# Attention with a Mish branch on one core: dense query and output rows by DMA, a third bank for ACT, patterns written over each other

## Chip, cores and metric

The kernel runs on one core of one Trainium2 chip. The metric is the device time of one execution in microseconds (us). Lower is better. PE is TensorE, ACT is ScalarE, DVE is VectorE, POOL is GpSimd, and SP is SyncE, which issues most of the DMAs.

## What is computed

The input x has 2048 tokens of 640 features. Branch A is softmax attention with 32 heads of 20 dimensions. Branch B is a dense layer to 1536 features, Mish, and a dense layer back. A gate per token mixes the two.

```python
g = _sigmoid((x * gate_w).sum(-1, keepdims=True))
qkv = (x @ wqkv)                                    # 640 -> 3 * 640, 32 heads of 20
scores = jnp.einsum("bhqd,bhkd->bhqk", q, k) * Dh ** -0.5
a = (softmax(scores) @ v) @ wo
h = x @ w1 + b1
b = (h * tanh(log1p(exp(-abs(h))) + where(h > 0, h, 0))) @ w2
out = g * a + (1 - g) * b
```

## The kernel before

**Tiles.** The tokens form 4 chunks c of 512 queries and 16 key tiles kt of 128 keys. The 32 heads form 8 groups g of 4 heads j. A unit is one (c, g, kt, j): a score matmul of 32 rows by 128 keys by 512 queries into one PSUM bank, then the exponential of 128x512 numbers. There are 2048 units. A head has 20 dimensions, and is held in KT and QT in a slot of 32 partitions, so that the four heads of a group use the four row strips of PE side by side. Groups run in this order: for chunks 0 and 1, group by group, both chunks in turn; then chunk 2 with all groups, then chunk 3.

**Who does the exponentials.** ACT takes two units at once (`emit_e`, line 1096), from two banks of PSUM into the ring ETS of 15 banks. The PSUM banks are two sets of three (0 to 2 and 3 to 5), of which the two first of each set hold ACT's scores; bank 6 (ACC) accumulates the PV products, and the banks FLEX (7, 5, 2) serve everything else. VectorE takes whole key tiles of four units: the conversion at line 1151 (`emit_x`) maps a score straight to the bits of a half-precision number, which approximates its exponential; then two more patterns with shifted bits are made from the first one (line 1178, 128x2048 each). The three patterns are multiplied with V in three weights, added up in ACC by `pv` (line 1298), with the weighted copies VS of V made by POOL (`weigh`, line 1201). A pattern occupies one of the lines LN, or a spare part of W2R, REG or HB, until PE has read it; the third pattern overwrites the first one where PE has already read that.

**The order of the work.** The program is written out at build time by a planner (`Plan.add`), with estimated costs of each instruction, one list for each engine. A step of the loop emits an exponential, the scores for two steps later (`compose`, `emit_s`), perhaps a conversion for VectorE (`x_block`, `emit_x`), the PV products that are ready (`emit_pv`, `emit_off`), pieces of projection tasks in between (`pick`, `put`), and filling matmuls where PE would be streaming too little (`fill_up`). `start_tile` decides whether VectorE begins a new tile: it needs free lines (one, and up to two more for unfinished patterns), VectorE not too far behind (BEHIND), and from slot CALM on; where a group has too little left, a tile is taken from the next group, its key tiles 0 and 1 only. `room` holds tiles back if VectorE's outstanding work is above LOAD times the time left. A slot is three units. Engines wait for each other by semaphores, in the order of their lists, and SP issues its DMAs in order as well.

**Projections.** Queries (`kq_task`, line 559) are computed group by group and chunk by chunk from weights that POOL has copied into padded columns (`pad`, line 537), five matmuls of 512 columns each, so that the four heads land in their 32-partition slots; VectorE evicts them (line 571). Keys of groups 1 to 7 are already computed in dense rows of 128 (`k_task`, line 613), evicted into a line of LN, written by DMA into the DRAM tensor KS (`shelve`, line 589), and read back in slots (line 605). The first queries and keys have code of their own (`first_keys`, line 681). V is at lines 707 and 734.

**Finishing a group.** After the last PV product of a group, `group_done` copies ACC to OUNG (line 1385), sends the row sums through three DMAs on SP (line 1388 into RR, a reciprocal at line 1392, lines 1393 and 1395 into BCT through the DRAM tensor SUMS), and multiplies OUNG by BCT (`times`, line 1355) into QT, over the queries of that group and chunk, which nobody needs any more. So the attention output lies in padded slots too: 4 x 32 partitions for a group. The output projection (`p_mm`, line 937) therefore takes 8 passes, one for each group, against Wo in padded rows (WOG), for each 128 tokens and each half of 320 columns. `load_wo` (lines 817 and on) fills WOG by nine DMAs when the last query task is done. For chunk 3, groups 0 to 5 are summed early (`part_task`, into PART), and groups 6 and 7 at the end (`late_mm`). VectorE mixes the result with branch B (line 943).

**Branch B.** The first layer is line 852, bias line 862, the tanh of Mish on ACT line 886, four VectorE pieces lines 903 to 906, the second layer lines 913 and 920.

## Time and profile before

| quantity | us |
|---|---|
| time before, median of 3 runs | 797.2 (796.22 to 799.04) |
| time of the profiled execution | 796.31 |
| span in that profile, first to last instruction | 794.5 |
| busy in it: PE / DVE / ACT / POOL | 774.7 / 681.7 / 772.9 / 146.2 |

The granted clock of PE was 0.999 in this execution. Groups of instructions are shown as line, engine, operation, output <- input, shapes, and xcount, then busy time, mean duration in ns, and the idle time of the engine ahead of them with what ended it. Durations overlap where an engine pipelines: 808 exponentials of a mean of 1119 ns keep ACT busy for 749.6 us. In timelines a row begins with start and length. In tables by stage each engine has its busy time and the count of its instructions, and the last three columns are the granted clock, the DMAs' share and GB/s. A "slice" of the span is a fortieth.

### The profile page before, as it was taken

What the parts mean: (1) busy time and instruction counts of PE and PEld (TensorE: products, weight loads), DVE (VectorE), ACT (ScalarE), POOL (GpSimd) and SP (SyncE); (2) the same over time, 40 slices, a digit from 0 to 9 for tenths busy, and PEclk for the clock granted to TensorE, in tenths of its full rate; (3) what the DMA queues carried; (4) which work ended last, traced back from release to release, by engine and by line L of the source; (5) the groups of instructions that cost most, each with busy time, mean ns of one, the idle gap of its engine ahead of it and who ended that gap; (6) DMA issues with size and microseconds to landing.
All of it is one profiled execution on the core that took longest, in us unless ns stands there. A gap on an engine that the chain in (4) does not pass through costs nothing.

```text
span 794.5 us, 16928 instructions
## 1 busy us (share of the span) xinstructions
PE 774.7 (98%) x7139; PEld 276.7 (35%) x7139; DVE 681.7 (86%) x1080; ACT 772.9 (97%) x839; POOL 146.2 (18%) x253
## 2 busy tenths in 40 slices
PE   8999999999999999999999999999999999999996
...
DMA packets 70020, 42.54 MB, mean 54 GB/s; under 512 B 20616, under 2 KB 65920, under 8 KB 69888
## 3 DMA queue, kind: packets, MB, share of 16 engines
...
q14 instruction: 26, 0.21, 0.1%
...
## 4 chain that ended last, share of the span: by engine, by line
ACT 67%; PE 27%; DVE 3%; DMA 1%; issue 0%; SPq 0%
ACT ETS L1096 64%; PE PS L1069 10%; PE PS L1298 8%; PE PS L559 2%; ACT REG L886 2%; PE PS L852 2%; PE PS L734 1%; PE PS L913 1%; DVE LN L1151 1%; PE PS L613 1%; PE PS L937 1%; DMA LN<-in_A_x_dram 1%; ACT W2R L886 1%; DMA RR<-OUNG 1%; PE PS L632 0%; DVE LN L1178 0%
## 5 line engine op out<-in xcount | busy, mean ns | idle before, releaser
L1096 ACT ACTIVATE ETS<-PS 128x1024 bf16<-128x1024 f32 x808 | 749.6, 1119 | 6.6 <-PE PS L1069 3.6
L1069 PE MATMUL PS<-QT,KT 32*128 32x512 bf16 (+1 forms) x2126 | 326.8, 377 | 11.0 <-ACT ETS L1096 7.3
L1151 DVE TENSOR_SCALAR LN<-PS 128x512 int16<-128x512 f32 x336 | 226.3, 683 | 25.7 <-PE PS L1069 24.0
L1201 POOL TENSOR_SCALAR VS<-V_all 128x84 bf16<-128x84 bf16 x224 | 131.1, 585 | 400.1 <-PE PS L1298 326.0
L1069 PEld LDWEIGHTS PS<-QT,KT 32*128 32x128 bf16 x2126 | 78.7, 91 | 245.0 <-ACT ETS L1096 215.1
L1298 PE MATMUL PS<-ETS,V_all 128*21 128x512 bf16 (+1 forms) x1664 | 154.0, 376 | 0.3 <-DVE V_all L715 0.3
L1178 DVE TENSOR_SCALAR LN<-LN 128x2048 int16<-128x2048 int16 x134 | 92.0, 690 | 3.4 <-PE PS L1298 2.4
L913 PE MATMUL PS<-W2R,HB 128*128 128x320 bf16 x384 | 76.9, 303 | 0.0
L1298 PEld LDWEIGHTS PS<-ETS,V_all 128*21 128x21 bf16 x1664 | 39.7, 90 | 64.0 <-issue 47.3
L1298 PE MATMUL PS<-LN,VS 128*21 128x512 f16 (+1 forms) x692 | 61.3, 375 | 0.0
L852 PE MATMUL PS<-XB,REG 128*128 128x256 bf16 x360 | 58.1, 275 | 0.0
L937 PE MATMUL PS<-WOQ,QT 128*128 128x320 bf16 x256 | 51.2, 303 | 0.4 <-DVE QT L1378 0.2
L559 PE MATMUL PS<-XB,WOQ 128*128 128x512 bf16 x155 | 48.7, 385 | 0.2 <-DVE V_all L744 0.2
L537 POOL COPY WOQ<-WOQ 128x400 bf16<-128x400 bf16 x16 | 8.3, 524 | 209.5 <-PE PS L559 204.8
L913 PEld LDWEIGHTS PS<-W2R,HB 128*128 128x128 bf16 x384 | 29.4, 97 | 37.2 <-issue 30.5
L852 PEld LDWEIGHTS PS<-XB,REG 128*128 128x128 bf16 x360 | 29.1, 97 | 24.2 <-issue 21.3
L862 DVE TENSOR_TENSOR HB<-PS,B1F 128x512 bf16<-128x512 f32 x48 | 32.7, 682 | 3.0 <-PE PS L852 3.0
L1151 DVE TENSOR_SCALAR REG<-PS 128x512 int16<-128x512 f32 x48 | 32.8, 684 | 1.5 <-PE PS L1069 1.4
L1298 PE MATMUL PS<-LN,V_all 128*21 128x512 f16 (+1 forms) x348 | 33.0, 376 | 0.0
L905 DVE SCALAR_TENSOR_TENSOR U<-U 128x1024 f32<-128x1024 f32 x24 | 29.4, 1224 | 0.1
L937 PEld LDWEIGHTS PS<-WOQ,QT 128*128 128x128 bf16 x256 | 19.5, 97 | 23.9 <-issue 17.4
L571 DVE CAST QT<-PS 128x512 bf16<-128x512 f32 x31 | 21.1, 681 | 7.6 <-PE PS L559 7.5
...
## 6 DMA issues: line engine op xcount, KB each, us to landing
...
```

Of the source, the lines that this page charges most:

```text
L559: return lambda e, bank: e.matmul(PS[:, bank, :], pads[:, b, f, :], xt(c)[:, f, :], start=(f == 0), stop=(f == NFT - 1))
L852: return lambda e, bank: e.matmul(PS[:, bank, i * HW:(i + 1) * HW], w1b(n1)[:, f, i * P:(i + 1) * P], xt(c)[:, f, cols], start=(f == 0), s ...
L862: ev = dve(lambda e: e.tensor_tensor(hb, PS[:, bank, :].rearrange("p (i t) -> p i t", i=2), bias, ALU.add), [last, *b1f, *guarded, *b_read ...
L905: piece(BROAD, lambda e: e.scalar_tensor_tensor(G, G, b, G, ALU.add, ALU.mult))
L913: return lambda e, bank: e.matmul(PS[:, bank, 0:HALF], HB[:, hc % 2, f, t * P:(t + 1) * P], W2[:, f, half * HALF:(half + 1) * HALF], start ...
L937: return lambda e, bank: e.matmul(PS[:, bank, 0:HALF], otn(c, g)[:, t * P:(t + 1) * P], WOG[:, g, half * HALF:(half + 1) * HALF], start=(g ...
L1069: op = pl.add("pe", lambda e, to=to, g=real(g), tile=tile, j=j, cols=cols, c=c, of_q=of_q: e.matmul(to[:, cols], KT[32 * j:32 * j + 32, g, ...
L1096: e_op[s] = pl.add("act", lambda e: e.activation(RING[:, p:p + n, :], scores(s)[:, 0:n, :], AF.Exp, scale=SCALE), [s_op[s], *(pv_slot[b] f ...
L1151: bank_free[bank] = x_ops[bank] = tile["op"] = dve(lambda e: e.tensor_scalar(dst, PS[:, bank, :], SCALE * ULPS, BASE, ALU.mult, ALU.add), ...
L1178: op = pl.add("dve", lambda e: e.tensor_scalar(to, src, SHADES[n], None, ALU.add), [last, *deps], cost=SHADE)
L1201: weighted[(c, g, k)] = n, [pl.add("pool", lambda e, i=i, n=n, src=src: e.tensor_scalar(VS[:, n, i, :, :], src, WEIGHTS[i + 1], None, ALU. ...
L1298: lasts[n] = pl.add("pe", lambda e, v=v, j=j, src=src[:, cols], of_q=of_q, begin=begin, end=end: e.matmul(PS[32 * j:32 * j + EW, ACC, of_q ...
```

## The change

1. **Queries.** Only group 0 is still computed with padded weights. The other 560 query rows are computed in dense rows, four tasks of 128 rows for each chunk, and the last 48 rows for two chunks side by side (`row_task`). VectorE evicts a task into one of two buffers (ROWS), and `send` issues one DMA on SP for each head's rows in it, into that head's slot of QT. POOL clears QT for groups 1 to 7 beforehand (seven memsets). A score matmul waits for the DMAs of its own head.
2. **Outputs.** `times` writes into one of two new buffers (ONS), and DMAs on SP move each head's 20 rows to their dense place in QT, split where they cross a multiple of 128. Wo is loaded dense (WOD, one DMA); the output projection takes 5 passes instead of 8. Groups 6 and 7 of chunk 3 keep padded rows (WOL, four DMAs and a memset by POOL); the early part of chunk 3 takes 4 passes instead of 6.
3. **Third bank.** `third` lets a step's exponential take three units where the third bank of its set is idle: with a conversion in the same step, or with VectorE behind ACT by THIRD; and not where projections press (CALLED).
4. **Patterns.** Each pattern after the first is made from the one before, in place if PE has read that one, or else in a new line if more than SPARED or KEPT lines are free. A new tile needs at most one line more than its own (NEED).
5. **Next group.** A tile of the next group may be any of its first four (BEFORE).
6. **Constants** of the planner are changed, among them CALM (21 to 10), LOAD (1.104 to 0.556), BEHIND (47.3 to 31.0), H_AT (172 to 150), PACKED (14 to 17) and the due times of the late queries.

```diff
-SLACK = 0.205
-LATER = 0.323
-FREE = 0.14
+SLACK = 0.225
+LATER = 1.181
+THIRD = 0.615
+CALLED = 0.642
+ROWED = 2
+SPARED = 0
+KEPT = 2
+NEED = 1
+BEFORE = 4
+FREE = 0.174
...
-AHEAD = 18
-BEHIND = 47.318
-MORE = 4.568
-PATIENCE = 2.597
-CATCH_UP = 289.517
+AHEAD = 19
+BEHIND = 30.956
+MORE = 6.787
+PATIENCE = 4.697
+CATCH_UP = 661.752
...
-SHIFT = 1.018
-LAG = 113
-WINDOW = 1.402
-CALM = 21
-PACKED = 14
-Q_AT = 70
-Q_STEP = 27.078
+SHIFT = 0.798
+LAG = 311
+WINDOW = 4.166
+CALM = 10
+PACKED = 17
+Q_AT = 84
+Q_STEP = 30.0
...
-SQ_STEP = 11
-H_AT = 172
+SQ_STEP = 13
+H_AT = 150
...
-LOAD = 1.104
+LOAD = 0.556
...
+    ONS = sb("ONS", [P, 2, CW], BF16)
...
-    PADQ = WOQ[:, NFT * D:].rearrange("p (b f c) -> p b f c", b=3, c=P)
-    WOG = WOQ[:, :].rearrange("p (g c) -> p g c", c=D)
+    PADQ = WOQ[:, NFT * D:NFT * (D + P)].rearrange("p (b f c) -> p b f c", b=1, c=P)
+    ROWS = [WOQ[:, NFT * (D + P) + n * CW:][:, 0:CW] for n in range(2)]
+    WOD = WOQ[:, 0:NFT * D].rearrange("p (f c) -> p f c", c=D)
+    WOL = WOQ[:, NFT * D:(NFT + 2) * D].rearrange("p (g c) -> p g c", c=D)
...
+            for g in range(1, NG):
+                blank_q[g] = pl.add("pool", lambda e, g=g: e.memset(QT[:, g, :].bitcast(FP32), 0.0), cost=1.2)
...
+            q_rows, row_free, row_read, q_sent = {}, {}, {}, [0]
+
+            def send(base, m, c, src, ev, n):
+
+                at = base
+                while at < base + m:
+                    head = at // DH
+                    g, j = divmod(head, HG)
+                    to = min(base + m, (head + 1) * DH)
+                    first, last = 32 * j + at - head * DH, 32 * j + to - head * DH
+                    name = f"qs{q_sent[0] % 8}"
+                    q_sent[0] += 1
+                    row_read[name] = op = pl.add("sp", lambda e, g=g, first=first, last=last, at=at, to=to: e.dma_start(
+                        QT[first:last, g, c * CW:(c + 1) * CW], src[at - base:to - base, :]),
+                        [ev, blank_q[g], row_read.get(name)], name, cost=0.5)
+                    wq_read.append(op)
+                    row_free.setdefault(n, []).append(op)
+                    some = q_rows.setdefault((g, c, j), [])
+                    some.append((to - at, op))
+                    if sum(rows for rows, _ in some) == DH:
+                        q_done[(g, c, j)] = [op for _, op in some]
+                    at = to
+
+            def row_task(name, parts, due):
+
+                base, m = (HD + P * name, P) if name < 4 else (HD + 4 * P, D - HD - 4 * P)
+
+                def mm(f, i, c):
+                    return lambda e, bank: e.matmul(
+                        PS[64 * i:64 * i + m, bank, :], WQ[:, f, base:base + m], xt(c)[:, f, :],
+                        start=(f == 0), stop=(f == NFT - 1), **(dict(tile_position=(0, 64 * i)) if m < P else {}))
+
+                def finish(bank, last):
+                    wq_read.append(last)
+                    n = row_turn[0] % 2
+                    row_turn[0] += 1
+                    for c in parts:
+                        x_read[c].append(last)
+                    ev = dve(lambda e: e.tensor_copy(ROWS[n], PS[:, bank, :]), [last, *row_free.pop(n, ())], WIDE)
+                    for i, c in enumerate(parts):
+                        send(base, m, c, ROWS[n][64 * i:64 * i + m, :], ev, n)
+                    return ev
+
+                return Task([mm(f, i, c) for f in range(NFT) for i, c in enumerate(parts)], PASS / len(parts), finish, due,
+                            lambda: [*(d for c in parts for d in xt_load[c]), w_load["wq"]], True)
+
+            row_turn = [0]
...
-                pieces = [(f"wo{j}", WOG[32 * j + 1:32 * j + 1 + DH, :, :], wo_v[j], 1.7) for j in range(HG)]
-                pieces.append(("wz", WOQ[0:P:32, :], none.to_broadcast([HG, NG * D]), 0.4))
-                pieces += [(f"wz{j}", WOQ[32 * j + 1 + DH:32 * j + 32, :], none.to_broadcast([32 - EW, NG * D]), 0.9)
-                           for j in range(HG)]
+                wo_v = A_wo[(NG - 2) * HD:, :].rearrange("(g j r) c -> j r g c", g=2, j=HG, r=DH)
+                blank = pl.add("pool", lambda e: e.memset(WOL.bitcast(FP32), 0.0), list(wq_read), cost=0.8)
+                pieces = [("wo", WOD, A_wo.rearrange("(f p) c -> p f c", p=P), 4.0)]
+                pieces += [(f"wo{j}", WOL[32 * j + 1:32 * j + 1 + DH, :, :], wo_v[j], 0.4) for j in range(HG)]
...
+        def p_mm(c, t, half, n, passes):
+
+            g, rows = passes[n]
+            w = WOL[:, g - (NG - 2), :] if rows == 0 else WOD[0:rows, g, :]
+            o = otn(c, g)[0:rows or P, t * P:(t + 1) * P]
             return lambda e, bank: e.matmul(
-                PS[:, bank, 0:HALF], otn(c, g)[:, t * P:(t + 1) * P], WOG[:, g, half * HALF:(half + 1) * HALF],
-                start=(g == groups[0]), stop=(g == groups[-1]))
+                PS[:, bank, 0:HALF], o, w[:, half * HALF:(half + 1) * HALF], start=(n == 0), stop=(n == len(passes) - 1))
...
+        all_rows = [(f, P) for f in range(NFT)]
+        early_rows = [(f, min(P, (NG - 2) * HD - f * P)) for f in range(-(-(NG - 2) * HD // P))]
+        late_rows = [(g, 0) for g in late]
...
+        def third(s, x):
+
+            bank = SLOT * (s % 2) + 2
+            if not fast or s < CALM or x and x[2] == bank or now["open"] and now["home"] == bank or now["rate"] >= CALLED:
+                return 0
+            free = bank_free.get(bank)
+            begin = max(pl.now["pe"], e_op[s - 2].t1 + HOP)
+            late = max(0.0, pl.now["dve"] - pl.now["act"])
+            if not x and late < THIRD or free is not None and free.t1 + HOP > begin:
+                return 0
+            held[bank] = s
+            return 1
+
+        def compose(s, j=None, more=0):
 
             some, js = [], [j]
-            while len(some) < width and order:
+            while len(some) < width + more and order:
...
-            def in_place(n):
-
-                return n == len(SHADES) - 1 and tile["read"]
-
             def ready(n):
+                if tile["read"]:
+                    return max([last, tile["read"]], key=lambda d: d.t1)
                 some = spare()
-                if in_place(n):
-                    return max([last, tile["read"]], key=lambda d: d.t1)
-                return max([last, *line_free[some[0]]], key=lambda d: d.t1) if some else stuck
+                if len(some) <= (SPARED if queue and tile["key"][:2] == queue[0][2][:2] else KEPT):
+                    return stuck
+                return max([last, *line_free[some[0]]], key=lambda d: d.t1)
 
             def piece(n):
                 def run():
-                    at, deps = (tile["at"], [tile["read"]]) if in_place(n) else grab()
+                    held, made = tile["held"], tile["items"][tile["held"]][0]
+                    if tile["read"]:
+                        at, deps = tile["at"], [tile["read"]]
+                        tile["read"], tile["held"] = None, n
+                    else:
+                        at, deps = grab()
                     to = line(at)
-                    op = pl.add("dve", lambda e: e.tensor_scalar(to, src, SHADES[n], None, ALU.add), [last, *deps], cost=SHADE)
+                    op = pl.add("dve", lambda e: e.tensor_scalar(
+                        to, src, SHADES[n] - SHADES[held], None, ALU.add), [made, *deps], cost=SHADE)
                     tile["items"].append((op, at))
                     if n == len(SHADES) - 1:
                         unshaded.remove(tile)
                         tile["shaded"] = op
-                        if at != tile["at"]:
-                            free(tile)
+                        free(tile)
...
-            need = sum(len(SHADES) - 1 - len(t["items"]) for t in unshaded)
+            need = sum(not t["read"] for t in unshaded)
             if (len(order) < 4 * HG or late + urgent + other >= BEHIND
-                    or len(spare()) < 1 + min(max(need, 0), len(SHADES) - 1)):
+                    or len(spare()) < 1 + min(need, NEED)):
...
-                kts = [kt for kt in range(2) if (c, g, kt) not in taken]
-                need = [k_done.get((real(g), 0)), q_done.get((real(g), c))]
+                kts = [kt for kt in range(BEFORE) if (c, g, kt) not in taken]
...
-                oung_free[0] = bc_read[0] = otn_done[(c, g)] = pl.add("dve", lambda e: e.tensor_tensor(
-                    otn(c, g), src, BC, ALU.mult), deps, cost=WIDE)
+                if c == NC - 1 and g in late:
+                    oung_free[0] = bc_read[0] = op = pl.add("dve", lambda e: e.tensor_tensor(
+                        otn(c, g), src, BC, ALU.mult), deps, cost=WIDE)
+                    otn_done[(c, g)] = [op]
+                    return
+                n = norm_turn[0] % 2
+                norm_turn[0] += 1
+                oung_free[0] = bc_read[0] = op = pl.add("dve", lambda e: e.tensor_tensor(
+                    ONS[:, n, :], src, BC, ALU.mult), [*deps, *norm_read.pop(n, ())], cost=WIDE)
+                norm_read[n] = otn_done[(c, g)] = []
+                for j in range(HG):
+                    at = g * HD + j * DH
+                    while at < g * HD + (j + 1) * DH:
+                        to = min((at // P + 1) * P, g * HD + (j + 1) * DH)
+                        first = 32 * j + 1 + at - g * HD - j * DH
+                        name = f"od{len(norm_read[n]) + 5 * n}"
+                        last_od[name] = move = pl.add("sp", lambda e, at=at, to=to, first=first: e.dma_start(
+                            otn(c, at // P)[at % P:at % P + to - at, :], ONS[first:first + to - at, n, :]),
+                            [op, last_od.get(name)], name, cost=0.5)
+                        norm_read[n].append(move)
+                        at = to
...
+            tasks.append(kq_task(0, 0, 1, slot_of(1, 0, 0) - 5))
+            lates = [lambda due, c=c: kq_task(0, 0, c, due) for c in range(2, NC)]
+            for i, g in enumerate((1, 2, 4, 5, NG - 1)):
+                if i < 4:
+                    tasks.extend(row_task(i, (c,), slot_of(c, g, 0) - PACKED - ROWED) for c in range(2))
+                    lates += [lambda due, i=i, c=c: row_task(i, (c,), due) for c in range(2, NC)]
+                else:
+                    tasks.append(row_task(i, (0, 1), slot_of(0, g, 0) - PACKED - ROWED))
+                    lates.append(lambda due, i=i: row_task(i, (2, 3), due))
+            tasks.extend(make(Q_AT + int(Q_STEP * n)) for n, make in enumerate(lates))
...
-                compose(step + 2, x and x[1][3])
+                compose(step + 2, x and x[1][3], third(step + 2, x))
...
```

109 lines of the change are left out of this document (55 added, 54 removed).

## Prediction

> **What bounds the kernel now.** First the busy line and the chain of what ended last, both on the page, and the costliest group.
>
> ```profile
> PE 774.7 (98%) x7139; PEld 276.7 (35%) x7139; DVE 681.7 (86%) x1080; ACT 772.9 (97%) x839; POOL 146.2 (18%) x253
> ...
> ACT 67%; PE 27%; DVE 3%; DMA 1%; issue 0%; SPq 0%
> ...
> L1096 ACT ACTIVATE ETS<-PS 128x1024 bf16<-128x1024 f32 x808 | 749.6, 1119 | 6.6 <-PE PS L1069 3.6 <-PE PS L1298 2.0
> ```
>
> PE and ACT are both near full, and the chain lies on ACT for two thirds. The wait view decides between them: which of the two stands still for the other?
>
> ```profile
> PEld PS L1069 <- ACT ETS L1096: 215.1, 638, 1.1
> ```
>
> The score matmuls' weight loads stand 215.1 us, in 638 places, until an exponential gives its banks back, while ACT waits 6.6 us for PE in all. PE is the follower. So I price ACT's work, from unbroken pieces of the chain in order of time (start, length, what).
>
> ```profile
> 12.92 54.28 ACT ETS L1096 x59
> ...
> 719.56 1.02 ACT REG L886
> 720.58 57.91 ACT ETS L1096 x63
> ```
>
> 57.91 / 63 = 0.919 us for one two-bank exponential, 0.46 us for a unit of 128x512. 808 of them are 742.6 us, and 24 Mish tanhs (8 blocks of 256 tokens, 3 each) at 1.02 us are 24.5: together 767.1 of the 794.5 us span. The other 27.4 us are the head (12.92, in which two exponentials, 1.8 us, already ran: 11.1), the 6.6 us of waits, and by difference 9.7 us of tail. The profiled execution took 796.3 us, 1.8 outside its span; the median before is 797.2, 0.9 above it.
>
> There are 4 x 8 x 16 x 4 = 2048 units. ACT does 1616, so VectorE does 432, which is 108 tiles of four heads. Time comes down almost only by moving tiles to VectorE, by making ACT's units cheaper, or by removing ACT's waits. How much room has VectorE? The busy time by stage (length, then PE, PEld, DVE, ACT, POOL):
>
> ```profile
> 0.00:12.92 12.92, 10.49 (x73) 5.38 (x73) 6.01 (x13) 4.98 (x8) 6.26 (x12) 1.00 0.99 185
> 12.92:40.00 27.08, 26.27 (x227) 9.81 (x227) 5.65 (x11) 27.08 (x30) 3.70 (x9) 1.00 0.45 109
> 40.00:100.00 60.00, 58.92 (x609) 21.15 (x612) 47.71 (x81) 59.90 (x66) 9.06 (x16) 1.00 0.17 49
> 100.00:140.00 40.00, 38.52 (x404) 16.20 (x401) 32.21 (x55) 36.04 (x40) 8.12 (x16) 1.00 0.11 36
> 140.00:340.00 200.00, 197.47 (x1770) 65.42 (x1769) 185.34 (x301) 198.99 (x217) 36.12 (x66) 1.00 0.20 59
> 340.00:740.00 400.00, 394.83 (x3482) 139.92 (x3479) 366.73 (x557) 399.52 (x434) 78.35 (x125) 1.00 0.17 49
> 740.00:784.50 44.50, 44.21 (x550) 17.20 (x550) 34.52 (x62) 44.50 (x49) 3.73 (x8) 1.00 0.06 18
> ```
>
> VectorE is idle 21.4 us before 40, 12.3 and 7.8 in the next two stages, 14.7 and 33.3 in the long ones, 10.0 near the end. So 68.1 us are idle between 40 and 740, and ACT loses 4.0 us in 100 to 140, the one stage where it visibly starves.
>
> **The change part by part.**
>
> *What a tile trades.* Rows of VectorE's timeline, a score conversion, a shifted pattern and a conversion in a row:
>
> ```profile
> 261.46 0.68 DVE L1151 TENSOR_SCALAR W2R<-PS 128x512 int16<-128x512 f32 x1
> 262.06 0.68 DVE L1178 TENSOR_SCALAR LN<-LN 128x2048 int16<-128x2048 int16 x1
> 262.66 0.68 DVE L1151 TENSOR_SCALAR W2R<-PS 128x512 int16<-128x512 f32 x1
> ```
>
> Starts are 0.60 us apart, so a tile (four conversions, two shifted patterns) costs VectorE 6 x 0.60 = 3.6 us and relieves ACT of two exponentials, 1.84 us.
>
> *Queries in rows, outputs in rows.* The groups concerned, and PE's own spacing:
>
> ```profile
> L937 PE MATMUL PS<-WOQ,QT 128*128 128x320 bf16 x256 | 51.2, 303 | 0.4 <-DVE QT L1378 0.2 <-DVE LN L1151 0.2
> L559 PE MATMUL PS<-XB,WOQ 128*128 128x512 bf16 x155 | 48.7, 385 | 0.2 <-DVE V_all L744 0.2
> ...
> L571 DVE CAST QT<-PS 128x512 bf16<-128x512 f32 x31 | 21.1, 681 | 7.6 <-PE PS L559 7.5
> ```
>
> ```profile
> 402.68 0.39 PE L1298 MATMUL PS<-ETS,V_all 128*21 128x512 bf16 x4
> 402.90 0.60 PE L1298 MATMUL PS<-LN,VS 128*21 128x512 f16 x8
> ...
> 404.07 0.72 PE L913 MATMUL PS<-W2R,HB 128*128 128x320 bf16 x4
> 405.90 0.45 PE L913 MATMUL PS<-W2R,HB 128*128 128x320 bf16 x2
> ```
>
> A second 512-column pass adds 0.60 - 0.39 = 0.21 us, a 320-column one (0.72 - 0.45) / 2 = 0.135. Query passes fall from 160 (the 155 and the first five) to 4 x 5 + 16 x 5 + 10 = 110: 50 x 0.21 = 10.5 us off PE. Output passes fall from 256 to 12 x 2 x 5 = 120, plus 8 x 4 and 8 x 2 for the last chunk, 168: 88 x 0.135 = 11.9 us. On PE, which follows, these 22.4 us buy nothing directly. They buy part of the 4.0 us that ACT loses in 100 to 140, where projections crowd the scores; I take 2, between 0 and 4. They also pay for two more PV passes (0.42 us) per tile. VectorE gains directly: query evictions fall from 32 to 1 + 3 + 16 + 2 = 22, 10 x 0.60 = 6.0 us.
>
> The price is DMAs. Query rows cross heads and go out as 7 + 7 + 8 + 7 + 3 = 32 pieces per chunk, 128 in all. Outputs go as 4 or 5 pieces per group, 36 per chunk, less 9 for the two groups kept padded: 135. Nearest row, the K pieces that the kernel already sends so:
>
> ```profile
> L589 SPq DMA_DIRECT2D KS<-LN x20: 314/336/1095, 36.0 to 282.1; - x20
> ...
> DMA to landing us min/median/max: 1.6/1.7/4.8
> ```
>
> Issue 0.336 us, landing 1.7. 263 x 0.336 = 88 us more on SP, spread over 772. Queries are due 19 slots before use and outputs are read by projections planned long after, so I cost both at nothing; the cover is that lead, and the norm chain, which uses the same queue, is the rival below.
>
> Seven clears of QT come onto POOL ahead of its first scaling of V:
>
> ```profile
> 0.72 0.20 POOL L492 MEMSET LN<- 128x128 bf16 x1 [0.29 <-POOLq L1818]
> ...
> 7.05 2.36 POOL L544 MEMSET V_all<- 128x512 bf16 x1
> ...
> 16.39 0.20 POOL L551 COPY REG<-GW 128x5 bf16<-128x5 bf16 x1 [4.67 <-DMA GW<-in_gate_w_dram]
> ...
> 33.74 2.92 POOL L1201 TENSOR_SCALAR VS<-V_all 128x84 bf16<-128x84 bf16 x6
> ```
>
> By elements, 1024 is 8 x 0.20 = 1.6 us by the dense clear and 2 x 2.36 = 4.7 by the strided one: 11 to 33 us after 16.6, ending at 28 to 50. These clears are dense, so I take 1.6. That ends about where the first tile now begins (below), at no cost; at 4.7 the first tiles would wait, at worst some 15 us of VectorE time, once, or 5 us by the balance below. The dropped Q pads give POOL time back, which it doesn't need.
>
> *Third bank.* What does a third bank cost in the same instruction? Two casts of ACT from PSUM give the slope:
>
> ```profile
> L656 ACT CAST XB<-PS 128x512 bf16<-128x512 f32 x2 | 1.2, 585 | 4.7 <-PE PS L672 4.6
> ...
> L656 ACT CAST KT<-PS 128x256 bf16<-128x256 f32 x1 | 0.4, 372 | 1.5 <-PE PS L660 1.5
> ```
>
> 213 ns for 256 columns, 0.426 us a bank. The two-bank exponential is then 0.852 plus 0.067 of its own, and a third bank costs 0.426 where it would cost 0.46: 0.033 us gained each. How often it is taken no row shows; between never and every second exponential (400, 13 us). The bank must be idle of conversions and projections, and the 432 conversions already sit beside half of the steps, so I take 150: 5 us.
>
> The Trainium skill (ScalarE: Activation LUTs, Rules for kernel authors) budgets about 0.3 us for every ACTIVATE beside 0.83 ns per element. Its slope agrees with the casts' 0.832; its fixed part would make two banks 1.15 us, where the run of 63 shows 0.919, so the fixed part is mostly hidden between exponentials in a row. By the page the 150 banks would save half of 0.3 us each, an estimated 22 us instead of 5.
>
> *Overwriting patterns, four early tiles, start at slot 10.* Before, an unfinished tile reserves up to two more lines, and a tile may begin only with a line left over; now a pattern that PE has read is shifted in place, so lines come free sooner and up to four tiles fill a group's end. What VectorE waits for in the long stages:
>
> ```profile
> DVE LN L1151 <- PE PS L1069: 13.2, 29, 1.6
> ```
>
> It is a conversion that had not been started in time, not a late result, so idle time is there to be had. The chain read, shift, read, shift now ties each pattern to PE, which can cost at a group's end. Beginning at slot 10 instead of 21 is 11 x 3 units x 0.46 = 15 us earlier, but PE is 97% busy there. Together I let VectorE win s = 30 us of idle time: 5 of the 21.4 before 40, 25 of the 68.1 after. Bounds: 0 and 75.
>
> *The sum.* With n more tiles, the span falls by d = 1.84 n + 5 (third bank). VectorE must fit 3.6 n - 6.0 into s - d, so n = (s + 6 - 5) / 5.44 = 31 / 5.44 = 5.7. Then d = 10.5 + 5 = 15.5, and with the 2 us of waits 17.5. From the profiled execution's 796.3 that is 778.8, from the median 779.7: **780 us**, about 114 tiles.
>
> **The rivals.**
>
> *VectorE no denser* (s = 0, third bank hardly taken, 1 us): n = 5 / 5.44 = 0.9, d = 2.7, no waits won: 794.5. For it: VectorE is already 92% busy in the two long stages, and the stricter load factor (0.556 for 1.104) holds tiles back in the second half. Against: the 6.0 us of evictions are gone whatever else happens. This is also the case that the edits are planned but not taken.
>
> *VectorE nearly full* (s = 60, third bank 8, waits 3): n = 58 / 5.44 = 10.7, d = 19.6 + 8 + 3 = 30.6: 766.5. For it: 68.1 us idle with no late input behind most of it. The page's 0.3 us would end there too (17 more than 17.5: 763); the run of 63 speaks against that.
>
> *SP's queue* (slower). The norm chain in VectorE's timeline, then in SP's:
>
> ```profile
> 254.31 0.68 DVE L1385 COPY OUNG<-PS 128x512 f32<-128x512 f32 x1
> ...
> 267.57 0.68 DVE L1355 TENSOR_TENSOR QT<-OUNG,BCT 128x512 bf16<-128x512 f32 x1
> ```
>
> ```profile
> 255.01 0.55 SPq L1388 DMA_DIRECT2D RR<-OUNG  x1
> ...
> 258.70 0.34 SPq L1393 DMA_DIRECT2D SUMS<-RR  x1
> 261.55 0.53 SPq L1395 DMA_DIRECT2D BCT<-SUMS  x1
> ```
>
> The chain holds OUNG 13.3 us; a group lasts about 772 / 31 = 24.9. SP works in order: a row DMA that waits for its VectorE result holds these three behind it. If a group's chain grows past 24.9, by more than 11.6 us, the next copy out of ACC waits, PV stops, and the ring of 15 banks holds ACT up. The added issues are 2.9 us per group, so it decides only when waiting in the queue is three times the issuing. At half of the groups, 1.6 us each, it costs 15 x 1.6 = 24 us: 797.2 - 17.5 + 24 = 803.7. The Trainium skill (DMA: Bandwidth & Descriptors, Rules for kernel authors) speaks against such pieces: transfers under 64 KB pay mostly overhead and are to be coalesced, and these have 20 KB or less. The 1.7 us landing of the K pieces agrees that the time is overhead; whether anyone waits for it is this rival.
>
> **How the numbers follow.** Forecast 0.55 (s from 15 to 45, the third bank and the waits between their bounds: 771 to 789); no denser 0.15; nearly full 0.15; SP's queue, or the clears at their upper bound, 0.15. About 0.3% (2.4 us) can be told from no change; 0.06 of the second case lies within it. Faster 0.55 + 0.15 + 0.09 = 0.79, same 0.06, slower 0.15. The range must keep 0.8: 767 leaves out half of the third case, 797 the slower one, so it is 767 to 797; the forecast's own is 771 to 789.
>
> **What would show it.** Right: L1151's count above 432 by some 20 or more; three-bank exponentials at about 1.35 us; VectorE's idle time between 40 and 740 near 40 us; ACT as full as now, with about 36.0 of 40 grown to 38 in 100 to 140. Query evictions 22, output matmuls 168. Wrong: ACT idle for PV or scores spread over the groups (queue or shift chain), SP rows long before the norm chain's three, the copy out of ACC waiting for OUNG, a tile count near 432, or POOL clears of 4 us with PE waiting for VS near 40.

## Result and the profile after

The changed kernel takes 829.2 us (median of 4 runs, 825.23 to 830.27); the kernel before took 798.1 us on the same chip (796.22 to 799.04). The ratio is 1.038, with a 95% interval of 1.034 to 1.043: 31 us slower, where 17 us faster was forecast. The profiled execution took 830.27 us, its span 828.3 us, with a mean granted clock of 0.964.

The page of the changed kernel: busy time, granted clock in fortieths of the span, the chain that ended last, and two groups. The exponential is now line 1170, the scores line 1143, the reciprocal of the row sums line 1494.

```profile
PE 757.0 (91%) x7053; PEld 266.7 (32%) x7087; DVE 703.6 (85%) x1118; ACT 760.6 (92%) x790; POOL 159.6 (19%) x262
...
PEclk9989989999997968998999999999999999999999
...
ACT 62%; PE 24%; DVE 6%; DMA 4%; SPq 1%; issue 1%; ACTq 0%; DVEq 0%
...
L1170 ACT ACTIVATE ETS<-PS 128x1024 bf16<-128x1024 f32 (+1 forms) x759 | 737.5, 1149 | 52.5 <-PE PS L1143 46.8
...
L1494 DVE RECIPROCAL RR<-RR 128x16 f32<-128x16 f32 x31 | 7.7, 248 | 27.8 <-DMA RR<-OUNG 27.8
```

Less work everywhere (PE 757.0 for 774.7, ACT 760.6 for 772.9), and a longer span. ACT's idle time ahead of exponentials went from 6.6 to 52.5 us. The reciprocal is new among the costly groups: VectorE stood 27.8 us for its input, and PE's clock fell in several slices of the first half. In the kernel before, VectorE stood 3.2 us for the row sums; the row of the DMA that brings them, there (ns min/median/max, first and last start), and who waited for it:

```profile
L1388 SPq DMA_DIRECT2D RR<-OUNG x31: 538/560/936, 42.3 to 765.8; - x31
...
  DVE RR L1392: 3.2, 4
```

ACT's groups with shapes kept apart:

```profile
L1170 ACT ACTIVATE ETS<-PS 128x1024 bf16<-128x1024 f32 x691 | 658.1, 1112 | 46.6 <-PE PS L1143 41.3 <-PE PS L1379 4.4
L1170 ACT ACTIVATE ETS<-PS 128x1536 bf16<-128x1536 f32 x67 | 102.4, 1541 | 5.9 <-PE PS L1143 5.5 <-PE PS L1379 0.3
```

With one exponential of a single unit, ACT did 691 x 2 + 67 x 3 + 1 = 1584 units, so VectorE did 464: 116 tiles, 8 more than before. A third bank costs 1541 - 1112 = 429 ns and was taken 67 times. ACT's work is 691 x 0.919 + 67 x 1.348 + 0.6 + 24.5 = 750.4 us, 16.7 less than the 767.1 before: the saving came. The waits by stage ate it (length, then PE, PEld, DVE, ACT, POOL, clock):

```profile
40.00:100.00 60.00, 54.26 (x573) 20.16 (x579) 49.37 (x87) 53.02 (x57) 10.23 (x18) 0.94 0.18 51
100.00:140.00 40.00, 32.98 (x303) 14.53 (x302) 28.03 (x47) 26.10 (x28) 8.15 (x18) 0.87 0.18 56
140.00:340.00 200.00, 182.69 (x1615) 63.72 (x1627) 170.36 (x274) 176.69 (x186) 33.07 (x54) 0.92 0.19 53
340.00:740.00 400.00, 377.82 (x3408) 128.21 (x3408) 368.56 (x561) 392.61 (x407) 77.29 (x119) 0.99 0.20 58
```

ACT is idle 7.0 + 13.9 + 23.3 + 7.4 = 51.6 us between 40 and 740, against 5.6 before, almost all of it ahead of 400. That is where the query pieces stand in SP's queue. Their row and that of the output pieces (ns min/median/max, first and last start):

```profile
L672 SPq DMA_DIRECT2D QT<-WOQ x128: 549/707/1701, 38.0 to 374.7; - x128
...
L1453 SPq DMA_DIRECT2D QT<-ONS x135: 558/714/932, 61.8 to 793.8; - x135
```

A piece of 20 rows holds SP for 0.71 us, twice the 0.336 of the K pieces of 128 rows. One spell shows what follows. Timelines of SP, VectorE, PE and ACT from 275 us on:

```profile
275.12 4.00 SPq L1453 DMA_DIRECT2D QT<-ONS  x5
279.18 5.20 SPq L672 DMA_DIRECT2D QT<-WOQ  x7
284.43 1.18 SPq L615 DMA_DIRECT2D KT<-KS  x2
285.65 0.48 SPq L865 DMA_DIRECT2D W2R<-in_B_w_dram  x1
286.17 0.58 SPq L1490 DMA_DIRECT2D RR<-OUNG  x1
286.79 0.65 SPq L865 DMA_DIRECT2D W2R<-in_B_w_dram  x1
287.50 6.11 SPq L672 DMA_DIRECT2D QT<-WOQ  x7
...
280.61 0.69 DVE L1487 COPY OUNG<-PS 128x512 f32<-128x512 f32 x1 [0.23 <-PE PS L1379]
...
291.60 0.25 DVE L1494 RECIPROCAL RR<-RR 128x16 f32<-128x16 f32 x1 [4.30 <-DMA RR<-OUNG]
...
291.42 1.25 PE L908 MATMUL PS<-XB,W2R 128*128 128x256 bf16 x5 [3.65 <-DMA W2R<-in_B_w_dram]
...
293.24 1.02 ACT L1170 ACTIVATE ETS<-PS 128x1024 bf16<-128x1024 f32 x1 [4.25 <-PE PS L1143]
```

Twelve pieces hold SP from 275.12 to 284.38. The copy to OUNG ended at 281.30, but its row sums leave SP at 286.17, 4.9 us later; in the rows that the prediction shows of the kernel before, the copy ended at 254.99 and they left at 255.01. Keys, weights of w1 and row sums leave together, behind the pieces; the weights land 5.7 us after 285.65, and PE stands 3.65 us and VectorE 4.30, each at the head of an in-order list. Over the 31 groups, the row sums left 37.0 us in all after their copy had ended (8.5 at most); in the kernel before it was 0.8 us. And it isn't over when they land. The same stretch by the granted clock:

```profile
283.00:287.50 4.50, 4.50 (x48) 1.30 (x46) 3.97 (x6) 4.50 (x6) 0.00 (x0) 1.00 0.16 46
287.50:291.40 3.90, 0.27 (x3) 0.00 (x0) 0.00 (x0) 1.50 (x2) 0.00 (x0) 0.93 0.79 193
291.40:304.60 13.20, 13.18 (x72) 3.75 (x72) 9.19 (x13) 6.92 (x7) 0.00 (x0) 0.50 0.19 55
304.60:311.00 6.40, 6.40 (x62) 2.27 (x58) 5.20 (x9) 6.30 (x7) 0.00 (x0) 1.00 0.07 21
```

After a stand of 3.65 us PE is granted half its clock for 13.2 us, though it is busy without a break: 72 matmuls in 13.2 us, where it did 48 in 4.5 before. ACT, full until then, is busy 6.92 of the 13.20. By the trace's clock records there are eight such spells ahead of 740 us, 58 us in all; the kernel before has none. Just ahead of six of them an engine had stood for a DMA that SP issues: VectorE for row sums ahead of those that begin at 133.8, 256.7, 290.8, 352.3 and 379.6 us, PE for keys ahead of 106.5. For PE's wait ahead of 51.9 the profile names no cause, and ahead of 318.1 PE waited only for ACT, 0.76 us at the longest.

### The profile page after: what moved, and what is told of

It reads as the page before. It is cut to its first block, busy times and chain, and to the rows that moved or that the text cites. A ratio compares the mean times of both kernels' runs of the same rounds, so it can differ in the third digit from the quotient of the medians.

```text
span 828.3 us, 17267 instructions
## 1 busy us (share of the span) xinstructions
PE 757.0 (91%) x7053; PEld 266.7 (32%) x7087; DVE 703.6 (85%) x1118; ACT 760.6 (92%) x790; POOL 159.6 (19%) x262
## 4 chain that ended last, share of the span: by engine, by line
ACT 62%; PE 24%; DVE 6%; DMA 4%; SPq 1%; issue 1%; ACTq 0%; DVEq 0%
ACT ETS L1170 60%; PE PS L1143 8%; PE PS L1379 7%; DMA RR<-OUNG 2%; ACT REG L942 2%; DVE LN L1228 2%; PE PS L969 1%; PE PS L792 1%; PE PS L908 1%; DVE LN L1258 1%; PE PS L688 1%; SPq L672 1%; PE PS L997 1%; PE PS L623 1%; DMA KT<-KS 1%
## 5 line engine op out<-in xcount | busy, mean ns | idle before, releaser
L1170 ACT ACTIVATE ETS<-PS 128x1024 bf16<-128x1024 f32 (+1 forms) x759 | 737.5, 1149 | 52.5 <-PE PS L1143 46.8
L1143 PE MATMUL PS<-QT,KT 32*128 32x512 bf16 (+1 forms) x2132 | 317.3, 388 | 48.9 <-ACT ETS L1170 33.0
L1228 DVE TENSOR_SCALAR LN<-PS 128x512 int16<-128x512 f32 x352 | 237.2, 684 | 41.8 <-PE PS L1143 39.8
L1283 POOL TENSOR_SCALAR VS<-V_all 128x84 bf16<-128x84 bf16 x240 | 145.4, 606 | 581.4 <-PE PS L1379 376.6
L1258 DVE TENSOR_SCALAR LN<-LN 128x2048 int16<-128x2048 int16 x159 | 108.9, 692 | 7.9 <-PE PS L1379 7.5
L1379 PE MATMUL PS<-LN,VS 128*21 128x512 f16 (+1 forms) x772 | 73.5, 390 | 3.5 <-DVE LN L1258 3.4
L997 PE MATMUL PS<-WOQ,QT 128*128 128x320 bf16 (+1 forms) x168 | 32.7, 302 | 0.3
L1494 DVE RECIPROCAL RR<-RR 128x16 f32<-128x16 f32 x31 | 7.7, 248 | 27.8 <-DMA RR<-OUNG 27.8
L1379 PEld LDWEIGHTS PS<-LN,VS 128*21 128x21 bf16 x772 | 17.8, 90 | 36.6 <-issue 19.7
L688 PE MATMUL PS<-XB,WOQ 128*128 128x512 bf16 (+1 forms) x88 | 25.1, 391 | 1.4 <-issue 0.7
L908 PE MATMUL PS<-XB,W2R 128*128 128x256 bf16 x120 | 22.3, 305 | 3.8 <-DMA W2R<-in_B_w_dram 3.6
```

The lines of the kernel that those rows point to most:

```text
L688: return lambda e, bank: e.matmul(PS[64 * i:64 * i + m, bank, :], WQ[:, f, base:base + m], xt(c)[:, f, :], start=(f == 0), stop=(f == NFT ...
L908: return lambda e, bank: e.matmul(PS[:, bank, i * HW:(i + 1) * HW], w1b(n1)[:, f, i * P:(i + 1) * P], xt(c)[:, f, cols], start=(f == 0), s ...
L997: return lambda e, bank: e.matmul(PS[:, bank, 0:HALF], o, w[:, half * HALF:(half + 1) * HALF], start=(n == 0), stop=(n == len(passes) - 1))
L1143: op = pl.add("pe", lambda e, to=to, g=real(g), tile=tile, j=j, cols=cols, c=c, of_q=of_q: e.matmul(to[:, cols], KT[32 * j:32 * j + 32, g, ...
L1170: e_op[s] = pl.add("act", lambda e: e.activation(RING[:, p:p + n, :], scores(s)[:, 0:n, :], AF.Exp, scale=SCALE), [s_op[s], *(pv_slot[b] f ...
L1228: bank_free[bank] = x_ops[bank] = tile["op"] = dve(lambda e: e.tensor_scalar(dst, PS[:, bank, :], SCALE * ULPS, BASE, ALU.mult, ALU.add), ...
```

## The experiments

**Theory:** the pieces hold SP's in-order queue, so that row sums, keys and weights leave late; VectorE and PE, also in order, stand for them, and PE's granted clock halves behind such stands. **Rivals:** the filling matmuls or the order of the work under the new constants; the outputs' pieces; the bytes of the pieces rather than their issue; or dense query rows as such, which change what PE and VectorE do and when.

Each run is set against the kernel before on its own chip, with medians of 796.3 to 797.1 us there, and 798.1 beside the changed kernel. So "over before" is the difference to that median; the changed kernel is 31.1 us over before.

| kernel | median us | ratio to before (95%) |
|---|---|---|
| before + dense queries (b_q) | 825.0 | 1.035 (1.028 to 1.042) |
| before + dense outputs (b_out) | 795.2 | 0.998 (0.997 to 1.000) |
| before + overwriting patterns (b_pat) | 814.3 | 1.022 (1.018 to 1.026) |
| changed, padded queries (padded_q) | 811.8 | 1.019 (1.014 to 1.024) |
| changed, padded outputs (padded_out) | 832.0 | 1.044 (1.039 to 1.049) |
| changed, both padded (no_rows) | 816.3 | 1.025 (1.019 to 1.031) |
| the same, old constants (no_rows_old) | 815.8 | 1.024 (1.022 to 1.027) |
| changed, WINDOW as before (window) | 848.8 | 1.065 (1.058 to 1.073) |
| changed, pieces planned at 0.73 (told) | 831.2 | 1.043 (1.038 to 1.049) |
| changed, one row in each piece (one_row) | 815.8 | 1.024 (1.018 to 1.031) |
| the same for queries only (one_row_q) | 818.2 | 1.027 (1.019 to 1.036) |
| changed, pieces issued by POOL (pool_pieces) | 803.8 | 1.010 (1.005 to 1.015) |
| before + 128 idle pieces (ballast) | 817.4 | 1.030 (1.023 to 1.036) |
| before + 256 idle pieces (ballast_2) | 901.8 | 1.132 (1.126 to 1.138) |
| changed, queries through DRAM (qs_raw) | 813.1 | 1.020 (1.017 to 1.022) |
| the same, constants fitted anew (qs_2) | 806.9 | 1.012 (1.010 to 1.014) |
| changed, padded queries, constants fitted anew (pq_2) | 793.2 | 0.994 (0.992 to 0.996) |

### Which row edit

**padded_q**: the queries of the kernel before in the changed kernel; no query pieces, no clears.

```diff
-                tasks.extend(row_task(i, (c,), slot_of(c, g, 0) - PACKED - ROWED) for c in range(2))
...
+                        tasks.append(kq_task(0, g, c, first - 5 if c < 2 else 70 + int(27.078 * (2 * g + c - 2))))
```

> The changed kernel with the padded queries of before (32 tasks of five 512-column passes, pads copied by POOL, no query rows by DMA); all else as changed. The queue theory says: the 128 query pieces of 0.71 us each stand ahead of the norm chain, the key fetches and the weight loads on SP in the first 390 us. Without them VectorE's 27.8 us of waits for the row sums fall to under 10, ACT's 47 us of waits for scores to under 15, the half-clock spells (granted clock 0.964) nearly go (over 0.985), and the time is 790 to 805 us. The dense-plan theory (VectorE packed to 116 tiles with no slack, so that any jitter stalls PE) says the waits stay above 30 us and the time stays above 815. The filler theory (the longer window lets PE stream too little) says the same, with the clock still near 0.965.

811.8 us, 14.8 over before: 16 us of the 31 went, but the time is outside the 790 to 805 of the theory. The reciprocal's wait fell to 0.6 us, the mean clock rose to 0.997, ACT's waits fell to 20.6. So the stalls for SP's DMAs are gone with the query pieces. But the time isn't back: 14.6 of the 20.6 us are waits for PV products, and 14.6 us of span follow the last exponential, where the changed kernel and the one before have less than 9.

**padded_out**: the outputs of the kernel before in the changed kernel.

```diff
-                if c == NC - 1 and g in late:
+                if True:
```

> The changed kernel with the padded output rows of before (no output pieces by DMA, Wo in padded rows, 256 output matmuls); query rows by DMA stay. The queue theory says: half of the 135 output pieces go from the first 390 us, while the 128 query pieces stay, so perhaps a third of the waits goes: 808 to 822 us, clock 0.97 to 0.985. If the query pieces alone matter it stays at 822 to 830. The dense-plan and filler theories: no gain, or slower by the 12 us of PE passes, 825 to 840.

832.0 us, ACT's waits 48.1, and 10.4 us for the last wait of all. The output pieces do add to the queue: without them the row sums left 20.9 us late in all instead of 37.0, and the reciprocal waited 10.1. But the time did not fall, so they alone are not the cause. They are issued behind the three DMAs of their own group's row sums, four or five for each group, and so stand ahead of what the next group needs.

**b_q** and **b_out**: one row edit alone on the kernel before, with its constants. (The diffs are parts 1 and 2 of the change.)

```diff
+                tasks.extend(row_task(i, (c,), slot_of(c, g, 0) - PACKED - ROWED) for c in range(2))
```

> The kernel before with the dense query rows by DMA alone (row tasks, 128 pieces on SP, seven clears by POOL), and its old constants. By the queue theory these pieces alone bring waits of VectorE for the row sums over 10 us and half-clock spells before 390 us: 803 to 815. By the prediction's account (10 fewer evictions, 10 us less of PE, pieces at nothing): 790 to 796.

```diff
+                    ONS[:, n, :], src, BC, ALU.mult), [*deps, *norm_read.pop(n, ())], cost=WIDE)
```

> The kernel before with the dense output rows by DMA alone (135 pieces on SP, 168 output matmuls for 256). The queue theory: pieces are issued just after the multiplication, when no norm chain is under way, so little harm: 792 to 800. If they hold the next key fetch and weight load up, 800 to 812.

Dense queries alone cost 28 us, more than the theory's 803 to 815, with ACT's waits at 27.8, the reciprocal's at 9.2, row sums 19.7 us late in all and 20.5 us of half clock ahead of the end. Some 6 us of the 28 are ACT's last wait (8.9 us for 2.5 before), which the next section puts down to the order. Dense outputs alone cost nothing (1.3 us faster), and their row sums left 1.1 us late in all. Of the two row edits it is the queries.

### Is it the other edits or the order

**no_rows**, **no_rows_old**: both row edits out of the changed kernel, with its constants and with those of before; **b_pat**: the overwriting patterns alone on the kernel before; **window**: one constant back.

```diff
-WINDOW = 4.166
+WINDOW = 1.402
```

> The changed kernel with padded queries and padded outputs of before, so without any row pieces, and with the third bank, the overwriting patterns, the four early tiles and the new constants. The run with padded queries alone took 811.8 and had 21 us of waits on ACT, part of them for PV. If the output pieces are the rest of the harm, this one is 795 to 806; if the new order and constants are, it stays at 806 to 818 or above, as PE also has 12 us more of output passes.

> As the run without row pieces, and with all constants of the planner as before (CALM 21, LOAD 1.104, window 1.402 and so on): only the third bank, the overwriting patterns and the four early tiles remain of the change. If these edits are good in themselves and the constants are fitted to dense rows, 785 to 795; if the overwriting patterns tie VectorE to PE at group ends, 800 or more with waits of ACT for PV.

```diff
-                    op = pl.add("dve", lambda e: e.tensor_scalar(to, src, SHADES[n], None, ALU.add), [last, *deps], cost=SHADE)
+                    op = pl.add("dve", lambda e: e.tensor_scalar(
+                        to, src, SHADES[n] - SHADES[held], None, ALU.add), [made, *deps], cost=SHADE)
```

> The kernel before with the overwriting patterns alone (each pattern made from the one before, in place once PE has read it; a tile needs one line more). If the chain of read and shift is the second cause (the run without row pieces had 14 us of VectorE waiting for PE ahead of a shift, 3.4 before, and 11 us of ACT waiting for PV), this one is 800 to 815 with the same waits. If it only frees lines, 788 to 796 with 2 to 6 more tiles than 108.

> The changed kernel with one constant of the planner put back: the window in which PE's streaming is counted for the filling matmuls, 1.402 instead of 4.166 us. The filler theory says: the half-clock spells go (clock over 0.99) and the time falls to 790 to 800. The queue theory says: PE stands for late inputs, which no filler behind the waiting matmul can mend; the waits of VectorE for the row sums stay at 20 to 30 us and the time within 815 to 835.

The window run put the lulls down to filling matmuls; it came out 20 us slower still, with waits of 70.9 us, and that theory fell as it was stated. The other three are slow for another reason than the changed kernel: the reciprocal waits 0.2, 3.2 and 0.2 us, and ACT waits less ahead of exponentials (18.6, 9.4 and 8.8 us; in no_rows 11.1 of it for PV products), but its last wait of all is long: 10.6 us in no_rows, and in no_rows_old and in b_pat:

```profile
ACT LN L1755 <- PE PS L954: 22.1, 1, 22.1
```

```profile
ACT LN L1755 <- PE PS L954: 24.0, 1, 24.0
```

It is 2.5 us in the kernel before and in the changed one. The order is written out by a planner, so each edit moves all the rest of it; here projections of the last chunk had not been placed beside exponentials, and stood behind the last one. These runs price an order that was not fitted to the edit; they can't price the edit. That holds in part for the row edits above as well, whose order moved too. The third bank and the early tiles were not run alone.

### What it is in the pieces

**told**: the planner is told the measured cost of a piece, for queries and outputs. **one_row**, **one_row_q**: the order unchanged, but each piece moves only its first row (in all pieces, or in the query pieces), so the rest of QT's rows are not written by them. **pool_pieces**: the order of every engine unchanged, but POOL issues the 263 pieces.

```diff
-                        [ev, blank_q[g], row_read.get(name)], name, cost=0.5)
+                        [ev, blank_q[g], row_read.get(name)], name, cost=0.73)
```

> The changed kernel, where the planner is told that a row piece costs 0.73 us on SP (the profile's median is 0.71) instead of 0.5; the pieces themselves stay, 263 of them. If the harm is that the planner doesn't see how long the queue is, its program now puts the reciprocal and the uses of keys later: waits of VectorE for the row sums under 12 us, time 785 to 805. If the harm is in the landing of the transfers (DMA engines busy with the pieces) rather than in their issue, the waits stay at 20 us or more and the time above 812.

```diff
-                        QT[first:last, g, c * CW:(c + 1) * CW], src[at - base:to - base, :]),
+                        QT[first:first + 1, g, c * CW:(c + 1) * CW], src[at - base:at - base + 1, :]),
```

> The changed kernel with the same program, instruction for instruction, but each of the 263 row pieces (queries and outputs) moves only the first of its rows instead of 4 to 20; so most query and output rows hold other data. It keeps the planner's order and takes away the pieces' weight. If the pieces' own cost (issue on SP and load on the DMA engines) starts the stalls, the issue falls below 0.5 us, VectorE's waits for the row sums fall from 27.8 to under 5 us, the half-clock spells (58 us before the tail) go, ACT's waits come down from 52 to under 15 us, and the time is 780 to 795. If the new order of work (dense plan) starts them, time stays over 815 with the same spells.

> As the run with one row for each piece, but for the 128 query pieces alone; the 135 output pieces move all their rows. If the query pieces do the harm: within 5 us of the run with one row in all. If it is the two together on one queue: halfway, 800 to 815, with waits for the row sums at 8 to 18 us. The dense-plan theory: over 815.

```diff
+    for op in fast.ops:
+        if op.slot and op.slot[:2] in ("qs", "od"):
+            op.eng = "pool"
```

> The changed kernel with the plan unchanged, but the 263 row pieces are issued by POOL instead of SP; every engine keeps its order, only SP's list is shorter and POOL's longer. If SP's issue time ahead of the norm chain, the key fetches and the weight loads is what remains of the harm (the run with one row for each piece still had 0.59 us of issue and 17 us of waits for the row sums), those waits fall under 5 us, the half-clock spells nearly go and the time is 785 to 800. If pieces that come late behind POOL's scaling of V are a new wait, PE waits for query pieces and the time is above 815.

Told the price, the planner did no better: the reciprocal waited 11.5 us instead of 27.8, but the product with BCT 15.0, and ACT 53.4. One row in each piece moves 263 rows instead of 4640, yet a piece still held SP for 0.587 us and the row sums left 26.5 us late in all; the reciprocal waited 17.3, and about 12 of the 31 us went, 9 with the query pieces alone. That is far from the 780 to 795 expected if the pieces' weight were all, and at the edge of the over 815 expected of the order alone; but half clock ahead of 740 fell from 58 to 37.5 us. With POOL as issuer, the plan being the same, 24 us went: 7.2 over before. The six executions lie between 799.7 and 808.1, and their median is above the expected 785 to 800. The reciprocal's wait in that kernel:

```profile
DVE RR L1494 <- DMA RR<-OUNG: 1.0, 2, 0.7
```

The clock was at half for 13.7 us ahead of the end instead of 58. What is left has a place too: at 64.05 us POOL issues seven pieces in 3.55 us, ahead of a scaling of V, and PE stands 2.27 us for VS. The row sums left 0.9 us late in all, for 37.0 in the changed kernel. So most of the loss is the place of the pieces in SP's in-order queue, and less their bytes. Where VectorE waited, 1.9 to 5.5 us passed from the issue of the row sums to the reciprocal, in the changed kernel and in the one before. Whether transfers behind pieces also land later in places, pool_pieces doesn't part from the issue, since it takes both off SP.

### Fewer pieces, and pieces alone

**qs_raw** sends dense query blocks through a DRAM buffer with 32-row slots: 20 writes, 28 reads and 4 fills with zeros for 128 pieces.

```diff
+                        "sp", lambda e: e.dma_start(to, ROWS[n][0:m, :]), [ev], f"qw{n}", cost=0.5)
...
+                    "sp", lambda e: e.dma_start(QT[:, g, c * CW:(c + 1) * CW], QS.ap()[c, g * P:(g + 1) * P, :]),
```

> The changed kernel with its constants, where a block of unpadded query rows (120 of them, six heads; the last block 80) leaves by one DMA write to a zero-filled DRAM buffer with 32-row slots, and each group's 128 padded rows come back by one read: 20 writes, 28 reads and 4 zero fills on SP in place of the 128 pieces, and VectorE's or GpSimd's seven clears of QT go. The outputs stay dense by their 135 pieces, the third bank, the patterns and the early tiles stay. Theory (the number of query pieces on SP's in-order queue is what costs; 128 x 0.71 = 91 us of SP go, 48 x 0.55 = 26 come): RECIPROCAL waits under 5 us (27.8 changed), the granted clock stands at half for under 8 us before the tail (about 55 changed), ACT's waits 8 to 22 us (52.5 changed), time 785 to 800. Rival (dense query rows as such: 22 evictions and their blocks fall badly for TensorE, and their way out does not matter): ACT's waits stay above 35 and the time above 812. Rival (the order that the planner lays out changes with every edit, so the tail is what varies): waits under 20, but exponentials end under 775 and a tail of more than 15 us behind them.

813.1 us, ACT's waits for exponentials 38.7: outside the theory's 785 to 800, inside the rival's numbers. The number of pieces, then, was too narrow a cause. But VectorE and PE again stood for DMAs that SP issues. Two rows of the wait view and one of PE's timeline in this kernel:

```profile
DVE RR L1488 <- DMA RR<-OUNG: 11.4, 7, 5.0
...
SPq L667 <- DMA QS<-WOQ: 43.3, 17, 7.7
```

```profile
272.99 0.61 PE L902 MATMUL PS<-XB,W2R 128*128 128x256 bf16 x2 [3.44 <-DMA W2R<-in_B_w_dram]
```

SP now issues little, but it waits 43.3 us in all for a block to land before it may read it back, and whatever stands behind waits too; the row sums left 11.8 us late in all. That these waits are what the 16.3 us over before come from is likely, but no run parts them from the order. To part SP from dense rows, **ballast** keeps the order of every other instruction of the kernel before and puts 128 pieces of 20 x 1 KB between scratch tiles behind its 28 query evictions; **ballast_2** puts 256. Nobody waits for them, and no row is dense.

```diff
+            while n < 128 * seen // 28:
+                j = (0, 1, 2, 3, 4, 6, 7)[n % 7]
+                dst = BAL[32 * (j % 4):32 * (j % 4) + DH, j // 4, :]
+                prior[j] = Op("sp", lambda e, dst=dst: e.dma_start(dst, BAL[32:32 + DH, 1, :]), [first, op, *([prior[j]] if j in prior else [])], f"ba{j}")
+                ops.append(prior[j])
+                n += 1
```

> The kernel before, whose instructions on TensorE, ScalarE and VectorE stand in the same order as ever, with 128 more DMAs on SP: after each of its 28 padded query evictions four or five copies of 20 rows x 1 KB from one scratch tile to another, which wait for that eviction and for which nobody waits (GpSimd clears the scratch once). Theory (the loss comes from pieces standing on SP's in-order queue ahead of row sums, key fetches and weights): issue about 0.6 to 0.75 us each, RECIPROCAL waits over 8 us (3.2 before), the granted clock at half for 5 us or more ahead of the tail (none before), ACT's waits for scores 15 to 40 us (2 to 7 before), time 806 to 830. Rival (the loss comes from what dense query rows do to TensorE's and VectorE's order, not from SP): within 4 us of before, ACT's waits under 12.

> The same with 256 such copies, nine or so after each eviction. Theory (SP's queue): at least as much again, 820 to 870 us, RECIPROCAL waits over 20. Rival (not SP): within 6 us of before.

128 idle pieces cost 20.8 us, 256 cost 105.3, more than the 820 to 870 expected. In ballast the piece's row and the waits of VectorE and ACT read:

```profile
L1790 SPq DMA_DIRECT2D BAL<-BAL x128: 706/707/1441, 44.5 to 379.2; - x128
```

```profile
DVE QT L1357 <- DMA BCT<-SUMS: 11.5, 7, 4.1
DVE RR L1394 <- DMA RR<-OUNG: 9.5, 8, 2.8
...
ACT ETS L1098 <- PE PS L1071: 21.8, 23, 4.1
```

The clock is at half for 20.5 us in it. In ballast_2 it is so for 109 us ahead of 740, and for 27.3 us more from 829.8 on, long after the last piece at 455 and behind no stand of PE over 0.53 us; the short ones add up to 1.05 of the 3.4 us ahead of it, and no DMA is shown behind them. The timelines of ballast_2 show the whole chain in one place:

```profile
394.38 13.16 SPq L1790 DMA_DIRECT2D BAL<-BAL  x17
407.58 0.48 SPq L815 DMA_DIRECT2D W2R<-in_B_w_dram  x1
408.12 0.73 SPq L1390 DMA_DIRECT2D RR<-OUNG  x1
...
416.49 0.25 DVE L1394 RECIPROCAL RR<-RR 128x16 f32<-128x16 f32 x1 [17.14 <-DMA RR<-OUNG]
...
417.35 1.46 PE L560 MATMUL PS<-XB,WOQ 128*128 128x512 bf16 x3 [16.72 <-DVE LN L1153]
```

Seventeen pieces, the row sums behind them (they leave at 408.12 and the reciprocal starts 8.4 us after), VectorE at its reciprocal, PE at a matmul whose bank VectorE has yet to empty. The rival of dense rows said within 4 and 6 us. Pieces alone, without a dense row, make these stalls, and pool_pieces, with all its dense rows, is rid of most of them: so dense rows fall as the cause of the changed kernel's stalls. That dense rows cost something besides, through the order, isn't excluded.

### Versions with a fitted order

**qs_2** is qs_raw, and **pq_2** is padded_q (dense outputs, third bank, patterns and early tiles kept), each with the planner's constants chosen anew.

```diff
-THIRD = 0.615
+THIRD = 0.933
...
-WINDOW = 4.166
+WINDOW = 1.646
```

> The same kernel with queries by the DRAM buffer, and the planner's constants chosen anew (THIRD 0.93, WINDOW 1.6, LOAD 0.76, H_AT 186 and the like), so that the order is fitted to the new DMAs. Theory: as without the new constants, and 5 to 10 us less, because the tail behind the last exponentials and the lulls shrink: 778 to 792, ACT's waits 5 to 18 us, granted clock 0.99 or more. If the piece count is not the cause, the time stays above 805 whatever the constants.

```diff
-THIRD = 0.615
+THIRD = 0.344
...
-LOAD = 0.556
+LOAD = 0.78
...
-H_AT = 150
+H_AT = 153
```

> The changed kernel with the queries padded as before (no query pieces at all: the projection writes padded rows, seven groups by four chunks), the outputs dense, third bank, patterns and early tiles kept, and the planner's constants chosen anew. With the changed kernel's own constants this took 811.8 us at a clock of 0.997. Theory (the cause of the loss is the query pieces, and what padded queries cost beyond that was only an order fitted to other work): 783 to 796, ACT's waits under 15 us. If padded queries lose by the 22.4 us of TensorE's work that they bring back, the time stays at 805 or more and PV and score matmuls are late for ACT throughout 100 to 340 us.

qs_2 reached 806.9 us, above its 778 to 792, with the reciprocal waiting 18.3 us in five places. pq_2 is faster than both kernels: 793.2 us, 0.6% under before. Its page:

```profile
L1126 ACT ACTIVATE ETS<-PS 128x1024 bf16<-128x1024 f32 (+1 forms) x778 | 743.9, 1141 | 9.4 <-PE PS L1099 8.5
```

778 exponentials, 52 of them with a third bank, make 1608 units, so 110 tiles; ACT waits 9.4 us, PE's clock is 0.992. Without query pieces on SP, the rest of the change with constants of its own gains, if little; what the edits give and what the constants, no run parts. No run reaches the forecast of 780.

## Why the prediction was wrong, point by point

**The step that failed is "263 x 0.336 = 88 us more on SP ... so I cost both at nothing".** It failed twice. The size: a piece took 0.71 us, so 128 x 0.707 + 135 x 0.714 = 187 us. The K pieces' row was taken as the nearest, but they are of 128 partitions and go to DRAM. Nearer in kind was RR<-OUNG, a copy within SBUF, at 0.560 in the row above and at 0.55 in the prediction's own lines for its rival; a piece of a single row still took 0.587. And the cover: I asked whether the readers of the pieces would wait, and hid the cost under their lead. The leads held: no wait of PE, VectorE or ACT is put down to a query piece. Those who waited were the DMAs behind the pieces in SP's queue, which have no lead: row sums (27.8 us of VectorE), a load of w1 (3.65 us of PE), keys (4.0 us of PE's weight loads).

**The rival "SP's queue" had the right place and the wrong victim.** It let the norm chain hold up OUNG, which has 11.6 us to spare for each group, and so was held to decide only at three times the issuing. The chain passes through VectorE earlier: the reciprocal stands in VectorE's list ahead of the conversions, so a late row sum stops VectorE at once, then PE, whose banks VectorE empties. In the twelve places where it waited there was no slack on this way. The rival's price, 24 us for 803.7, was thus too small; and the range ended at 797 because it left this rival out, with no bound of the issue cost in it.

**A stall of PE was priced at its own length.** Nothing in the trace of before shows the price, for PE's clock did not fall there ahead of the last microseconds. After a stand of 3.65 us PE ran 13.2 us at half clock. The Trainium skill (TensorE: Matmul & The Clock Gate, Why this matters for your kernels) warns of idle gaps of PE over some 3 us, after which the clock drops to half: for this spell the trace agrees. But ahead of the other seven the longest stand was 0.52 to 2.98 us, so shorter ones were enough. For the way back it asks for some 4 us of continuous work; here the spell lasted through 13.18 us of it, so the measurement decides.

**What the pieces cost in all.** Taking them off SP in the same plan gave back 24 us (31.1 over before against 7.2). It may be more, for POOL's own list suffers from them. Putting 128 on the kernel before cost 20.8. The balance of the profile: ACT's work -16.7, its waits +45.9, the remaining 4.6 not traced further, together the 33.8 us between the spans of 794.5 and 828.3.

**Right:** the price of ACT's work, which fell by 16.7 us where the sum had 15.5; the third bank's slope (0.429 for 0.426), 22 query evictions and 168 output matmuls. **Right by luck:** the tiles, 116 for 114 forecast, 14.7 us for 10.5. The sum fitted them into 30 us of idle time that VectorE would win. But its idle time grew, from 794.5 - 681.7 = 112.8 us to 828.3 - 703.6 = 124.7, and the tiles, which the plan had placed at build time, fitted because the span grew. In pool_pieces, the same plan with most stalls gone, idle time was 798.4 - 702.9 = 95.5: 17 us won of the 30.

**Smaller misses.** The third bank was taken 67 times, not 150: 2.0 us, not 5. The 2 us of waits to be won in 100 to 140 became 9.9 lost (26.10 busy of 40 for 36.04). POOL's clears took 0.95 us each, not 1.6, and no engine is shown waiting for them. VectorE's idle time between 40 and 740 was not 40 us but 10.6 + 12.0 + 29.6 + 31.4 = 83.7, for it stood 24.6 us longer for row sums than before; in pool_pieces it was 54.6.

**Small transfers.** The rule against them that the rival named held for the queries' 20 KB pieces, but the 135 of the outputs alone cost nothing (b_out). The K pieces, whose 1.7 us landing the prediction took as agreeing with it, are no small transfers: 16 of the 20 carry 128 KB. What does agree is that a piece of 1 KB took the same 1.7 us to land (one_row). The Trainium skill (DMA: Bandwidth & Descriptors, Issuing engines are not separate DMA queues) counts the time that a sequencer takes to start a DMA as usually small beside the DMA; here the turns in SP's list were most of the loss, as pool_pieces shows with 24 of 31 us.

**Open:** how much of the remaining 7 us of pool_pieces, and of qs_2's 10, is the order and how much is stalls; pool_pieces still has 22.7 us of ACT's waits for exponentials, where the kernel before has 6.6. And why half clock lasts 3.4 us in some places and 13.7 in others.
